# Row-half transposes and a new order of work inside the query steps of a fused attention and two-layer kernel

## The chip, the cores and the metric

One Trainium2 chip, and of it one core. The time is device microseconds of one launch; the kernel before took 869.48 us (median of 3 runs, 868.94 to 870.9).

## The reference, cut to what matters

Linear attention with random features, and behind it two feed-forward layers on the 2304 tokens that come out. The change lies in the attention, in the part that works on the queries.

```python
batch, n_heads, seq, head_dim, n_features = 4, 8, 576, 64, 128
def phi(x):                                   # x is q or k, times 64 ** -0.25
    proj = einsum('bhsd,md->bhsm', x, omega)
    sq = sum(x * x, axis=-1, keepdims=True) / 2
    h = proj - sq
    return exp(h - max(h, axis=-1, keepdims=True)) / sqrt(128)
q_p, k_p = phi(q), phi(k)
kv = einsum('bhsm,bhsd->bhmd', k_p, v);  z = sum(k_p, axis=2)
out = einsum('bhsm,bhmd->bhsd', q_p, kv) / (einsum('bhsm,bhm->bhs', q_p, z) + 1e-6)
x = out.transpose(0, 2, 1, 3).reshape(2304, 512)
x = leaky(x @ moe_w_in) @ moe_w_out           # d_ff = 2048, a slope for each hidden unit
return relu(x @ moe2_w_in) ** 2 @ moe2_w_out
```

## The kernel before, in words

The 2304 tokens are 18 tiles of 128. The key steps come first (`k_step`, 18 and a tail), then the query steps (`q_step`, numbered s = 0 to 20), then the two layers, which fill the time from about 136 us on. Every engine's instructions run in the order in which the code records them, so the order of lines in `q_step` is the order on each engine. Between the query steps' own instructions `make()` records pieces of the preparation of the layers' weights (on ACT, DVE, POOL and the DMA queues). In the last steps, from s = 18 (`DRAIN`), `more()` adds the first products of the layers; before that it does nothing.

A query step is a software pipeline over four tiles of tokens. In step s:

- DVE divides the products of tile z = s - 3 by their denominator (L723 to L725, `rec` and `xn`).
- PE transposes the 8 heads' features of tile v = s - 2, `eq`, 128x128 each: the first four into the PSUM bank `tt[0]`, the next four into `tt[1]` (L735). ACT copies each bank to SBUF (`t`, L738, two copies of 512 columns).
- ACT takes the exponentials of tile s - 1 (L637, eight of 128 columns).
- PE projects tile s (L612): eight products with a contraction of 64 rows, which alternate between the upper and the lower half of PE's rows. DVE takes the maxima over them (L625, `greatest`, 1024 columns).
- PE transposes the divided outputs `xn` of tile z into `tt[0]` (L754, four of 128x128), and DVE copies them into `x` (L755, 512 columns).
- PE sums the squares of tile s into 8 columns of `tt[1]` (L619, 64 output rows at a time). DVE makes of these and the maxima the bias of the next step's exponentials (L631 and L632, `bias`).
- PE multiplies tile v's transposed features with the sums over keys (L767, 16 products of 64 output rows, into `o`).

`tt[0]` and `tt[1]` are one PSUM bank each and are never doubled: the transposes of `eq`, those of `xn` and the sums of squares take turns in them, and each must wait until ACT or DVE has read what stood there. The projections have two sets of banks in turn, `o` has one.

Of the kernel before, what the change touches and what calls it, by code (L numbers as in the profile page):

```python
# [9 lines left out]
F32 = mybir.dt.float32  # L10
# [9 lines left out]
P = 128  # L20
B, H, S, D = 4, 8, 576, 64
T = B * S
NT = T // P
NP = H // 2
# [3 lines left out]
KC = DM // P  # L28
# [3 lines left out]
W = D + 1  # L32
# [22 lines left out]
DRAIN, DRAINED = 18, 6  # L55
# [5 lines left out]
def tile_performer_moe(ctx, tc, qt, kt, qn, kn, vn, omt, w1i, w1o, al, w2i, w2o, out):  # L61
    nc = tc.nc
# [467 lines left out]
    def xpart(t0, n):  # L530

        b = t0 // NB
        assert (t0 + n - 1) // NB == b
        return x[:, b, :, t0 - b * NB:t0 - b * NB + n]

    def attention():
        with ExitStack() as ac:
            ka = ac.enter_context(tc.tile_pool(name="ka", bufs=1, side="right"))
            ld = ac.enter_context(tc.tile_pool(name="ld", bufs=4, side="right"))
            wk = ac.enter_context(tc.tile_pool(name="wk", bufs=3, side="right"))  # L540
# [11 lines left out]
            tt = [po.tile([P, 512], F32, name=f"t{j}") for j in range(2)]  # L552
# [5 lines left out]
            def projections(i):  # L558

                j = i % 2  # L560
                if halves_only[j]:
                    halves_only[j].close()
                    halves_only[j] = None
                    pools[j] = (pbc, ac)[j].enter_context(
                        tc.tile_pool(name=("pb", "pa")[j], bufs=1, space=PSUM, reuse_waits="tile", **sides[j]))
                return pools[j].tile([P, 2, NP, M], F32, name="h")

            def products():
                return po.tile([P, 2, 512], F32, name="o")

            HP = P // 2
            HALVES = (slice(0, HP), slice(HP, P))
            om = ka.tile([P, M], F32, name="om")
            pick = ka.tile([P, 2], F32, name="pick")
            ident = ka.tile([P, P], F32, name="ident")
            kvr = ka.tile([P, B, H, W], F32, name="kvr")
# [13 lines left out]
            def load(key):  # L590
                which, i = key
                raws[key] = raw = ld.tile([P, NP, P], F32, name="raw")
                nc.sync.dma_start(out=raw, in_=(kt if which == "k" else qt)[i])
# [5 lines left out]
            def square(key):  # L599
                sqts[key] = wk.tile([P, NP, P], F32, name="sqt", bufs=2)  # L600
                nc.gpsimd.tensor_tensor(out=sqts[key], in0=raws[key], in1=raws[key], op=ALU.mult)
# [6 lines left out]
            def project(key, pj):  # L608

                for c in range(NP):  # L610
                    for j, rows in enumerate(HALVES):
                        nc.tensor.matmul(pj[j][:, c, :] if isinstance(pj, list) else pj[:, j, c, :], raws[key][rows, c, :], om[rows], start=True, stop=True)  # L612

            def square_sums(key, o):

                sqt = sqts.pop(key)
                for c in range(NP):
                    for rows in HALVES:
                        nc.tensor.matmul(o[rows, 2 * c:2 * c + 2], sqt[:, c, rows], pick,  # L619
                                         start=True, stop=True, skip_group_check=True)  # L620
                return o.rearrange("p (c j) -> p j c", j=2)

            def greatest(pj, n=2):
                mx = sm.tile([P, 2, NP], F32, name="mx")[:, :n]
                nc.vector.reduce_max(out=mx, in_=pj, axis=AX.X)  # L625
                return mx

            def bias(mx, nsq, n=2):

                nb = sm.tile([P, 2, NP], F32, name="nb")[:, :n]  # L630
                nc.vector.tensor_tensor(out=mx, in0=nsq, in1=mx, op=ALU.add)  # L631
                nc.vector.tensor_tensor(out=nb, in0=nsq, in1=mx, op=ALU.subtract)  # L632
                return nb

            def feature(pj, nb, e):
                for c in range(NP):
                    nc.scalar.activation(out=e[:, c, :], in_=pj[:, c, :], func=AF.Exp, bias=nb[:, c:c + 1])  # L637
# [28 lines left out]
            has = lambda i, n=NT: 0 <= i < n  # L666
# [44 lines left out]
            fs, ns, qpj, qnb, outs = {}, {}, {}, {}, {}  # L711

            def q_step(s, make=lambda: None, more=lambda: None):
                k = next(ahead, None)
                if k:
                    load(k)

                z = s - 3
                if has(z):
                    o = outs.pop(z)[:, :, 0:NP * W].rearrange("p j (h w) -> p j h w", w=W)  # L720
                    ns[z] = xn = wk.tile([P, NP, 2, D], F32, name="xn", bufs=2)
                    rec = sm.tile([P, 2, NP, 1], F32, name="rec")
                    nc.vector.tensor_scalar(out=rec, in0=o[:, :, :, D:], scalar1=eps, scalar2=None, op0=ALU.add)  # L723
                    nc.vector.reciprocal(out=rec, in_=rec)
                    nc.vector.tensor_tensor(  # L725
                        out=xn.rearrange("p c j d -> p j c d"), in0=o[:, :, :, 0:D],
                        in1=rec.to_broadcast([P, 2, NP, D]), op=ALU.mult)
                make()

                v = s - 2  # L730
                if has(v):
                    e = fs.pop(v)
                    for j in range(2):
                        for c in range(NP):
                            nc.tensor.transpose(tt[j][:, c * P:(c + 1) * P], e[:, j, c], ident)  # L735
                    t = [wk.tile([P, NP, P], F32, name=f"t{j}", bufs=2) for j in range(2)]
                    for j in range(2):
                        nc.scalar.copy(out=t[j], in_=tt[j].rearrange("p (c n) -> p c n", n=P))  # L738
                if has(s - 1):
                    fs[s - 1] = e = wk.tile([P, 2, NP, M], F32, name="eq", bufs=2)  # L740
                    for j in range(2):
                        feature(qpj[s - 1][:, j], qnb[s - 1][:, j], e[:, j])
                    del qpj[s - 1], qnb[s - 1]
                more()
                if has(s):
                    qpj[s] = projections(s)
                    project(("q", s), qpj[s])
                    mx = greatest(qpj[s])

                if has(z):  # L750
                    xt = tt[0].rearrange("p (c n) -> p c n", n=P)
                    xn = ns.pop(z).rearrange("p c j d -> p c (j d)")
                    for c in range(KC):
                        nc.tensor.transpose(xt[:, c, :], xn[:, c], ident)  # L754
                    nc.vector.tensor_copy(out=xpart(z * P, P), in_=xt)  # L755
                more()

                if has(s):
                    nsq = square_sums(("q", s), tt[s % 2 if s < 2 else 1][:, 0:H])
                    qnb[s] = bias(mx, nsq)  # L760
                if has(v):
                    outs[v] = o = products()
                    for j in range(2):
                        for c in range(NP):
                            for rows in HALVES:
                                b = (v * P + rows.start) // S
                                nc.tensor.matmul(o[rows, j, c * W:(c + 1) * W], t[j][:, c, rows], kvr[:, b, 2 * c + j],  # L767
                                                 start=True, stop=True, skip_group_check=True)
                if has(s + 1):
                    square(("q", s + 1))  # L770

# [33 lines left out]
            for j in range(3):  # L805
                k_step(NT + j)
                q_step(j)
                if j < 2:
                    onward(1, BLOCKS - 1)
                else:  # L810
                    ask(2, BLOCKS - 1)
# [12 lines left out]
            for s in range(3, NT + 3):  # L824
                def make():
                    for n, at in zip((B11, B21, B12, B22), CASTS):
                        if s == at:
                            cast(0, n, as_it_is)
                        elif s == at + 1:
                            rest(0, n, as_it_is)  # L830
                    if s == HELD:
                        held.pop()()
                    if s in APART:
                        apart(APART[s])
                    if s == CAST:

                        gate[0] = len(UNITS) * 4
                        ask(2, 0)
                    blk = 0 if s >= CAST else BLOCKS - 1
                    upto(STAGES + MADE.get(s, 0), 2, blk)  # L840
                    if s == DRAIN:
                        apart(T4)
                    if s == DRAIN + 1:
                        cast(0, T2, in_place)
# [433 lines left out]
    def room_of(k, n):  # L1278
        return x[:, k].rearrange("p c n -> p (c n)")[:, n * NB:(n + 1) * NB]
# [145 lines left out]
    for c in range(3):  # L1425
        o = room_of(k, M65)[:, c * QW:(c + 1) * QW]
# [45 lines left out]
```

## Time and profile before

| | us |
|---|---|
| median of 3 runs | 869.48 (868.94 to 870.9) |
| profiled execution, its own time | 868.84 |
| its span, first to last instruction | 867.0 |
| query steps 3 to 17 in it, from step 3's first transpose to step 18's | 63.10 to 126.87 |
| PE busy | 862.3 (99%) |
| DVE busy | 677.6 (78%) |
| ACT busy | 520.6 (60%) |

The busy shares are over the whole span, of which the layers are five sixths. For the change only the query steps count, and of them the order of PE, DVE and ACT inside one step. A PE that counts as busy can still lose time between instructions of different shapes, since the recorded matmuls overlap each other.

### The profile page before, as it was taken

The page shows a single profiled execution, that of the slowest core. Times are in us where ns is not written, and L with a number is a line of the kernel's source. Part 1 is how long each engine was busy: PE and PEld are TensorE (multiplying, and loading weights), DVE is VectorE, ACT ScalarE, POOL GpSimd, SP SyncE. Part 2 cuts the span into 40 slices and gives each one's busy share as a digit, 9 for nine tenths or more (in the row PEclk, how much of TensorE's full clock was granted, in tenths as well). Part 3 has the DMA queues.
Part 4 walks back from the last instruction along what each step waited for, and adds up shares of the span by engine and source line. Part 5 has one row for each costly group of instructions (what it writes and reads, how often), then busy time and mean ns, then how long its engine had stood idle before and what let it go on. Part 6 is the DMA issues. An engine that isn't in the chain of part 4 may idle for free.

```text
span 867.0 us, 17497 instructions
## 1 busy us (share of the span) xinstructions
PE 862.3 (99%) x6803; PEld 799.1 (92%) x6803; DVE 677.6 (78%) x1126; ACT 520.6 (60%) x1027; POOL 97.3 (11%) x138
## 2 busy tenths in 40 slices
PE   9999999999999999999999999999999999999998
PEld 7998889999999999999999999998899988999888
DVE  5778987998996776888778865669956699757686
ACT  6889897999877666667767633335333355333442
POOL 6742432111101000010000000000000000000000
PEclk9999999999999999999999999999999999999999
DMA  7744306899838999839999957687797687876874
GB/s 260 218 151 149 112 14 232 290 323 332 313 125 273 395 381 379 314 112 380 394 406 383 360 197 226 217 293 252 255 309 250 207 311 257 300 253 224 299 254 153
DMA packets 88530, 228.76 MB, mean 264 GB/s; under 512 B 6784, under 2 KB 19456, under 8 KB 83456
## 3 DMA queue, kind: packets, MB, share of 16 engines
q1 hardware_dynamic: 78880, 192.21, 62.6%
q0 software_dynamic: 9216, 33.56, 11.4%
q10 hardware_dynamic: 352, 1.87, 0.6%
q8 instruction: 54, 0.88, 0.4%
q14 instruction: 28, 0.23, 0.1%
HBM read 170.47 MB, written 57.15 MB: 263 GB/s over the span
## 4 chain that ended last, share of the span: by engine, by line
PE 94%; ACT 2%; DVE 2%; DMA 1%; issue 0%; ACTq 0%; DVEq 0%
PE h L861 29%; PE y L1057 21%; PE sumc L1251 11%; PE spare L861 10%; PE suma L1251 9%; PE h L612 4%; PE t L735 2%; PE t L619 2%; PE o L767 2%; PE o L658 2%; PE t L754 1%; ACT e L637 1%; DMA x<-in_w2i 1%; DVE xl L498 0%; PE t L606 0%
## 5 line engine op out<-in xcount | busy, mean ns | idle before, releaser
L861 PE MATMUL h<-xh,w 128*128 128x384 f32 x984 | 276.2, 337 | 0.1
L861 PEld LDWEIGHTS h<-xh,w 128*128 128x128 f32 x984 | 180.4, 188 | 2.9 <-ACT c L886 0.4
L1057 PE MATMUL y<-gh,w 128*128 128x512 f32 (+1 forms) x768 | 174.1, 337 | 0.1
L861 PE MATMUL h<-xl,w 128*128 128x384 f32 x492 | 165.3, 336 | 0.0
L1057 PEld LDWEIGHTS y<-gh,w 128*128 128x128 f32 x768 | 130.6, 188 | 12.6 <-ACT gh L886 0.4
L1057 PE MATMUL y<-gl,w 128*128 128x512 f32 (+1 forms) x384 | 102.2, 337 | 0.0
L1266 ACT CAST gh<-g 128x768 fp32r<-128x768 f32 x72 | 56.9, 833 | 74.1 <-PE suma L1251 33.1
L861 PEld LDWEIGHTS h<-xl,w 128*128 128x128 f32 x492 | 92.5, 188 | 2.1
L861 PE MATMUL spare<-xh,w 128*128 128x384 f32 x336 | 91.0, 334 | 0.0
L1268 DVE TENSOR_TENSOR gl<-g,gh 128x768 fp32r<-128x768 f32 x72 | 65.7, 953 | 14.3 <-PE suma L1251 7.1
L1251 PE MATMUL sumc<-w,gh 128*128 128x512 f32 (+1 forms) x296 | 76.6, 379 | 0.0
L1057 PEld LDWEIGHTS y<-gl,w 128*128 128x128 f32 x384 | 67.1, 188 | 9.7
L886 ACT ACTIVATE s<-h,sg_sb 128x384 f32<-128x384 f32 x69 | 40.0, 580 | 37.8 <-PE h L861 37.6
L861 PEld LDWEIGHTS spare<-xh,w 128*128 128x128 f32 x336 | 61.3, 188 | 0.2
L1251 PEld LDWEIGHTS sumc<-w,gh 128*128 128x128 f32 x296 | 52.8, 189 | 9.3
L625 DVE TENSOR_REDUCE mx<-h 128x8 f32<-128x1024 f32 (+1 forms) x38 | 44.4, 1167 | 18.1 <-PE h L612 17.4
L899 DVE SCALAR_TENSOR_TENSOR c<-h,sg_sb,s 128x384 f32<-128x384 f32 x69 | 42.4, 615 | 18.0 <-PE h L861 7.2
L861 PE MATMUL spare<-xl,w 128*128 128x384 f32 x168 | 56.1, 334 | 0.0
L904 DVE SCALAR_TENSOR_TENSOR c<-c,al_sb 128x768 f32<-128x768 f32 x48 | 48.6, 1012 | 8.4 <-ACT c L886 8.4
L1251 PE MATMUL suma<-w,gh 128*128 128x512 f32 x216 | 52.4, 391 | 0.0
L886 ACT ACTIVATE gh<-c,sg_sb 128x768 fp32r<-128x768 f32 x48 | 45.0, 937 | 8.1 <-DVE c L904 7.9
L910 DVE SCALAR_TENSOR_TENSOR gl<-c,sg_sb,gh 128x768 fp32r<-128x768 f32 x48 | 48.5, 1011 | 0.0
(138 smaller groups left out, 1500.8 us busy)
## 6 DMA issues: line engine op xcount, KB each, us to landing
w<-k SPq DMA_DIRECT2D x99, 512.0 KB, 5.1
w<-k SPq DMA_DIRECT2D x39, 1024.0 KB, 4.9
w<-k SPq DMA_DIRECT2D x26, 896.0 KB, 7.7
k<-ms SPq DMA_DIRECT2D x36, 512.0 KB, 7.0
k<-w SPq DMA_DIRECT2D x16, 512.0 KB, 6.5
x<-in_w2i POOLq DMA_DIRECT2D x16, 512.0 KB, 6.5
x<-in_w2o POOLq DMA_DIRECT2D x16, 512.0 KB, 7.2
ms<-in_w1o POOLq DMA_DIRECT2D x14, 512.0 KB, 5.8
```

The lines of the kernel that those rows point to most:

```text
L612: nc.tensor.matmul(pj[j][:, c, :] if isinstance(pj, list) else pj[:, j, c, :], raws[key][rows, c, :], om[rows], start=True, stop=True)
L619: nc.tensor.matmul(o[rows, 2 * c:2 * c + 2], sqt[:, c, rows], pick, start=True, stop=True, skip_group_check=True)
L625: nc.vector.reduce_max(out=mx, in_=pj, axis=AX.X)
L861: nc.tensor.matmul(out, w[:, u, a, cs], tiles[v, b][:, kc], start=start and kc == 0 and j == 0, stop=stop and kc == 1 and j == 2, skip_gro ...
L886: nc.scalar.mul(out=to, in_=of, mul=sg_sb[:, 2 * p + i:2 * p + i + 1])
L899: nc.vector.scalar_tensor_tensor(out=c[:, ts], in0=b, scalar=sign, in1=s, op0=ALU.mult, op1=ALU.add)
L904: nc.vector.scalar_tensor_tensor(out=c, in0=c, scalar=slope, in1=c, op0=ALU.mult, op1=ALU.max)
L910: nc.vector.scalar_tensor_tensor(out=gl[:, i], in0=c, scalar=sign, in1=gh[:, i].bitcast(F32), op0=ALU.mult, op1=ALU.subtract)
L1057: nc.tensor.matmul(y[a0 // 512][:, a0 % 512:a0 % 512 + a1 - a0], u[:, i, c * P:(c + 1) * P], v[:, i, ts], start=first and j == 0 and a0 % ...
L1251: nc.tensor.matmul(to[c] if v == 3 or banks else to[c][:, :QW], (l if v == 2 else h)[:, r, c * P:(c + 1) * P], both(r) if v == 3 else w[:, ...
L1266: nc.scalar.copy(out=h[:, r], in_=f[:, r])
L1268: nc.vector.tensor_tensor(out=l[:, r], in0=f[:, r], in1=h[:, r].bitcast(F32), op=ALU.subtract)
```

## The change

Four edits, all in the query steps; the key steps keep their form (the squares of keys are still summed in halves).

1. Up to s = 17 the transposes of `eq` and of `xn` are made in row halves: each 128x128 transpose becomes two with a contraction of 64 rows, whose outputs are 128x64. The upper halves go to `tt[0]`, the lower ones to `tt[1]`, in turn. ACT still copies both banks, and DVE copies `xn`'s out of both, 256 columns each.
2. The products with the sums over keys stand in front of the sums of squares.
3. The query's sums of squares are made in quarters (32 output rows) where they were made in halves.
4. The transposes of `xn` and the copies of them into `x` stand in front of the maxima.

From s = 18 on the forms and the order are as before.

```diff
             def square_sums(key, o):
 
                 sqt = sqts.pop(key)
+                n = P // 2 if key[0] == "k" else P // 4
                 for c in range(NP):
-                    for rows in HALVES:
+                    for rows in (slice(r, r + n) for r in range(0, P, n)):
                         nc.tensor.matmul(o[rows, 2 * c:2 * c + 2], sqt[:, c, rows], pick,
                                          start=True, stop=True, skip_group_check=True)
...
                     e = fs.pop(v)
+                    t = [wk.tile([P, 512], F32, name=f"t{j}", bufs=2) for j in range(2)]
                     for j in range(2):
                         for c in range(NP):
-                            nc.tensor.transpose(tt[j][:, c * P:(c + 1) * P], e[:, j, c], ident)
-                    t = [wk.tile([P, NP, P], F32, name=f"t{j}", bufs=2) for j in range(2)]
+                            if s < DRAIN:
+                                at = slice((j * NP + c) * HP, (j * NP + c + 1) * HP)
+                                for r, rows in enumerate(HALVES):
+                                    nc.tensor.transpose(tt[r][:, at], e[rows, j, c], ident[rows, rows])
+                            else:
+                                nc.tensor.transpose(tt[j][:, c * P:(c + 1) * P], e[:, j, c], ident)
                     for j in range(2):
-                        nc.scalar.copy(out=t[j], in_=tt[j].rearrange("p (c n) -> p c n", n=P))
+                        nc.scalar.copy(out=t[j], in_=tt[j])
+
+                    def turned(j, c, r):
+
+                        if s < DRAIN:
+                            return t[r][:, (j * NP + c) * HP:(j * NP + c + 1) * HP]
+                        return t[j][:, c * P + r * HP:c * P + (r + 1) * HP]
...
                     project(("q", s), qpj[s])
+
+                if has(z):
+                    xn = ns.pop(z).rearrange("p c j d -> p c (j d)")
+                    if s < DRAIN:
+                        xt = [tt[r][:, 0:2 * P].rearrange("p (c n) -> p c n", n=HP) for r in range(2)]
+                        for c in range(KC):
+                            for r, rows in enumerate(HALVES):
+                                nc.tensor.transpose(xt[r][:, c], xn[rows, c], ident[rows, rows])
+                        for r in range(2):
+                            nc.vector.tensor_copy(out=xpart(z * P + r * HP, HP), in_=xt[r])
...
+                more()
+                if has(s):
                     mx = greatest(qpj[s])
 
-                if has(z):
-                    xt = tt[0].rearrange("p (c n) -> p c n", n=P)
-                    xn = ns.pop(z).rearrange("p c j d -> p c (j d)")
-                    for c in range(KC):
-                        nc.tensor.transpose(xt[:, c, :], xn[:, c], ident)
-                    nc.vector.tensor_copy(out=xpart(z * P, P), in_=xt)
-                more()
-
-                if has(s):
-                    nsq = square_sums(("q", s), tt[s % 2 if s < 2 else 1][:, 0:H])
-                    qnb[s] = bias(mx, nsq)
                 if has(v):
                     outs[v] = o = products()
...
-                                nc.tensor.matmul(o[rows, j, c * W:(c + 1) * W], t[j][:, c, rows], kvr[:, b, 2 * c + j],
+                                nc.tensor.matmul(o[rows, j, c * W:(c + 1) * W], turned(j, c, r), kvr[:, b, 2 * c + j],
                                                  start=True, stop=True, skip_group_check=True)
+                if has(s):
+                    nsq = square_sums(("q", s), tt[s % 2 if s < 2 else 1][:, 0:H])
+                    qnb[s] = bias(mx, nsq)
```

On PE, step 10 of the kernel before, from the transposes of `xn` to the next step's transposes of `eq` (`t_129` is `tt[0]`, `t_130` is `tt[1]`, `t_1944` and `t_1945` are ACT's copies of them):

```order
L754 MATMUL t_129<-ident,xn 128x128 [waits DVE_49,Activation_49]
L754 MATMUL t_129<-ident,xn 128x128 x3
L619 MATMUL t_130<-pick,sqt 64x2 [waits Activation_49,Pool_49]
L619 MATMUL t_130<-pick,sqt 64x2 x7
L767 MATMUL o<-kvr,t_1944 64x65 [waits PE_49]
L767 MATMUL o<-kvr,t_1944 64x65 x7
L767 MATMUL o<-kvr,t_1945 64x65 x8
L735 MATMUL t_129<-ident,eq 128x128 [waits DVE_49,Activation_49]
L735 MATMUL t_129<-ident,eq 128x128 [waits Activation_49] x3
L735 MATMUL t_130<-ident,eq 128x128 [waits DVE_49,Activation_49]
```

The sixteen products stand between the sums of squares and the next transposes, and of those the first that writes `tt[1]` is the fifth.

The same place of the changed kernel (`t_2115` and `t_2116` are ACT's copies there):

```order
L768 MATMUL t_129<-ident,xn 128x64 [waits DVE_49,Activation_49]
L768 MATMUL t_130<-ident,xn 128x64 [waits Activation_49]
...
L786 MATMUL o<-kvr,t_2115 64x65 [waits PE_49]
L786 MATMUL o<-kvr,t_2116 64x65
...
L620 MATMUL t_130<-pick,sqt 32x2 [waits DVE_49,Pool_49]
L620 MATMUL t_130<-pick,sqt 32x2 x15
L740 MATMUL t_129<-ident,eq 128x64 [waits Activation_49]
L740 MATMUL t_130<-ident,eq 128x64 [waits DVE_49]
```

The sums of squares now stand last in the step, the second transpose of the next step writes `tt[1]` and waits for DVE, and the second transpose of `xn` writes `tt[1]` too and waits for ACT.

On DVE, step 11 of the kernel before, from its last instruction for the weights or the casts (L498) to the next step's `xn`:

```order
L498 TENSOR_TENSOR xl_1384<-x,xh_1383 128x768
L625 TENSOR_REDUCE mx<-h 128x8 [waits PE_49]
L755 COPY x<-t_129 128x4x128 [waits PE_49,Activation_49]
L631 TENSOR_TENSOR mx<-t_130,mx 128x8 [waits DVE_49,PE_49,Activation_49]
L632 TENSOR_TENSOR nb<-t_130,mx 128x8 [waits DVE_49]
L723 TENSOR_SCALAR rec<-o 128x8 [waits PE_49]
```

The maxima wait for the projections and run while PE makes the transposes of `xn`; the copy comes after them.

The same place of the changed kernel:

```order
L498 TENSOR_TENSOR xl_1416<-x,xh_1415 128x768
L770 COPY x<-t_129 128x4x64 [waits PE_49,Activation_49]
L770 COPY x<-t_130 128x4x64 [waits PE_49,Activation_49]
L626 TENSOR_REDUCE mx<-h 128x8
L632 TENSOR_TENSOR mx<-t_130,mx 128x8 [waits DVE_49,PE_49]
L633 TENSOR_TENSOR nb<-t_130,mx 128x8 [waits DVE_49]
```

The two copies wait for the transposes of `xn`, and the maxima stand behind them.

## Rows read from the trace of the kernel before

**Rows 1.** The page: span; busy time by engine; granted TensorE clock in 40 slices.

```profile
span 867.0 us, 17497 instructions
PE 862.3 (99%) x6803; PEld 799.1 (92%) x6803; DVE 677.6 (78%) x1126; ACT 520.6 (60%) x1027; POOL 97.3 (11%) x138
PEclk9999999999999999999999999999999999999999
```

**Rows 2.** Busy time in steps 3 to 17; first line names the columns.

```profile
core 0: us, PE busy (x) PEld busy (x) DVE busy (x) ACT busy (x) POOL busy (x), PEclk, DMA share, GB/s
63.10:126.87 63.77, 63.77 (x1144) 55.92 (x1140) 56.01 (x123) 56.28 (x167) 22.66 (x21) 1.00 0.31 105
```

**Rows 3.** Chain of waits, 108 to 118 us: start, length, engine and work.

```profile
by line: PE o L767 25.4%; PE h L612 21.8%; PE t L735 20.5%; PE t L754 17.6%; PE t L619 16.9%
...
109.94 1.02 PE t L735 x8
110.96 1.09 PE h L612 x16
112.05 0.59 PE t L754 x4
112.64 0.56 PE t L619 x16
113.20 0.99 PE o L767 x32
```

**Rows 4.** Timeline of PE: transposes that begin steps 2, 3 and 18.

```profile
59.42 1.11 PE L735 MATMUL t<-ident,eq 128*128 128x128 f32 x8
...
63.10 1.09 PE L735 MATMUL t<-ident,eq 128*128 128x128 f32 x8
...
126.87 1.09 PE L735 MATMUL t<-ident,eq 128*128 128x128 f32 x8
```

**Rows 5.** Timeline of PE, step 10: start, length, line, weights' shape, moving shape.

```profile
92.86 1.09 PE L735 MATMUL t<-ident,eq 128*128 128x128 f32 x8
93.89 1.16 PE L612 MATMUL h<-om,raw 64*128 64x128 f32 x16
94.98 0.66 PE L754 MATMUL t<-ident,xn 128*128 128x128 f32 x4
95.56 0.63 PE L619 MATMUL t<-pick,sqt 128*64 128x2 f32 x16
96.05 1.13 PE L767 MATMUL o<-kvr,t 128*64 128x65 f32 x32
97.11 0.44 PE L735 MATMUL t<-ident,eq 128*128 128x128 f32 x2
```

**Rows 6.** Timeline of DVE, step 10.

```profile
93.42 0.69 DVE L725 TENSOR_TENSOR xn<-o,rec 128x512 f32<-128x512 f32 x1
94.02 0.95 DVE L498 TENSOR_TENSOR xl<-x,xh 128x768 fp32r<-128x768 f32 x1
95.09 1.23 DVE L625 TENSOR_REDUCE mx<-h 128x8 f32<-128x1024 f32 x1
96.23 0.68 DVE L755 COPY x<-t 128x512 f32<-128x512 f32 x1
96.83 0.16 DVE L631 TENSOR_TENSOR mx<-t,mx 128x8 f32<-128x8 f32 x1
97.02 0.17 DVE L632 TENSOR_TENSOR nb<-t,mx 128x8 f32<-128x8 f32 x1
97.23 0.17 DVE L723 TENSOR_SCALAR rec<-o 128x8 f32<-128x8 f32 x1
```

**Rows 7.** Timeline of ACT, step 10.

```profile
93.56 1.07 ACT L738 COPY t<-t 128x512 f32<-128x512 f32 x2 [0.38 <-PE t L735]
94.52 2.19 ACT L637 ACTIVATE eq<-h,nb 128x128 f32<-128x128 f32 x8
```

**Rows 8.** Groups of DVE and ACT, 63 to 127 us: count, busy us, mean ns.

```profile
L625 DVE TENSOR_REDUCE mx<-h 128x8 f32<-128x1024 f32 x15 | 18.4, 1225 | 5.6 <-PE h L612 4.9
L755 DVE COPY x<-t 128x512 f32<-128x512 f32 x15 | 10.2, 681 | 0.0
...
L738 ACT COPY t<-t 128x512 f32<-128x512 f32 x30 | 16.1, 589 | 6.7 <-PE t L735 6.7
```

More of the change, by code (lines that the diff above doesn't have):

```diff
@@ L747, in q_step @@
                     project(("q", s), qpj[s])
-                    mx = greatest(qpj[s])
                 if has(z):
-                    xt = tt[0].rearrange("p (c n) -> p c n", n=P)
                     xn = ns.pop(z).rearrange("p c j d -> p c (j d)")
-                    for c in range(KC):
-                        nc.tensor.transpose(xt[:, c, :], xn[:, c], ident)
-                    nc.vector.tensor_copy(out=xpart(z * P, P), in_=xt)
+                    if s < DRAIN:
[5 more added lines that the diff above has]
+                            nc.vector.tensor_copy(out=xpart(z * P + r * HP, HP), in_=xt[r])
+                    else:
+                        xt = tt[0].rearrange("p (c n) -> p c n", n=P)
+                        for c in range(KC):
+                            nc.tensor.transpose(xt[:, c, :], xn[:, c], ident)
+                        nc.vector.tensor_copy(out=xpart(z * P, P), in_=xt)
                 more()
                 if has(s):
-                    nsq = square_sums(("q", s), tt[s % 2 if s < 2 else 1][:, 0:H])
-                    qnb[s] = bias(mx, nsq)
+                    mx = greatest(qpj[s])
                 if has(v):
@@ L764, in q_step @@
                         for c in range(NP):
-                            for rows in HALVES:
+                            for r, rows in enumerate(HALVES):
                                 b = (v * P + rows.start) // S
-                                nc.tensor.matmul(o[rows, j, c * W:(c + 1) * W], t[j][:, c, rows], kvr[:, b, 2 * c + j],
+                                nc.tensor.matmul(o[rows, j, c * W:(c + 1) * W], turned(j, c, r), kvr[:, b, 2 * c + j],
                                                  start=True, stop=True, skip_group_check=True)
+                if has(s):
+                    nsq = square_sums(("q", s), tt[s % 2 if s < 2 else 1][:, 0:H])
+                    qnb[s] = bias(mx, nsq)
                 if has(s + 1):
```

## The prediction

> **What bounds the kernel now.** I read the page first: one core, PE busy 99% of 867.0 us, its clock granted in full in every slice [rows 1]. That says little on the query steps, so I cut out steps 3 to 17. There PE has no idle time at all, DVE is busy 56.0 and ACT 56.3 of 63.8 us [rows 2]. The chain of waits in this stretch is PE alone, phase after phase [rows 3]. From step 3's first transpose to step 18's are 63.77 us [rows 4], 15 equal periods of 4.25 us.
>
> One period by the starts of its phases [rows 5], all in us: transposes of eq 1.03 (92.86 to 93.89), projections 1.09, transposes of xn 0.58, sums of squares 0.49, products 1.06. So PE sets the period. But DVE has little room beside it: the maxima start at 95.09, 0.11 after the projections' phase ends, and maxima, copy into x and the bias's two operations end at 97.19; the transposes that overwrite what the copy and the bias read begin at 97.11 in tt[0] and about 0.45 later in tt[1] [rows 5, 6]. The maxima run beside xn's transposes, and the copy and the bias beside the products. That cover is what the new order moves.
>
> **The change, part by part.** The phases give the price of a transpose: eight take 1.03 and four 0.58, so one takes 0.1125 and each phase has a constant of 0.13. The projections show row halves of the same weight shape: 8 products, recorded as 16 rows of 64x128, in 1.09 [rows 5]. If the two halves run side by side that is 8 pairs at 0.12 with the same constant. A pair of row halves then costs what one whole transpose costs, and edit 1 gains nothing by itself except constants: transposes, projections and xn's transposes have one shape now, so of the four changes of shape in a step three are left, at about 0.13 to 0.19 each.
>
> Edit 3: the sums of squares take 0.031 a row with 2 moving columns, the products 0.033 with 65 [rows 5]; so time goes with the 64 weight columns. No row shows 32 columns. Bounds: the phase of 0.49 falls to 0.25 if four run side by side at half the time, or doubles to 0.98 if only two do. Taken is 0.25 to 0.49, and it will not matter, since PE waits for DVE at this place in any case.
>
> What matters is the order. I follow one period from T = 0, the start of the first transpose of eq into tt[1]. It waits for the bias's second operation, since the bias reads the sums in tt[1]; before, the first transpose that did so was the fifth, and the products stood between.
>
> - ACT's first copy started 0.70 after the first of four transposes into its bank (92.86 to 93.56) [rows 5, 7]. Now a bank is complete only with the seventh or eighth pair, 3 to 4 pairs later: 1.10.
> - ACT's two copies take 1.07 [rows 7]: 2.17. With 0.05 for the waking (the first copy before starts that long after its last transpose ended) 2.22. Here the second xn transpose, which writes tt[1], may start. PE has been ready since about 1.8 (8 and 8 pairs at 0.1125): a new wait of 0.4. Before, xn's transposes wrote tt[0] alone, which ACT's first copy frees early.
> - From the projections' start to the maxima's start are 1.20 for 8 pairs (93.89 to 95.09) [rows 5, 6]. Without four pairs, without the last tt[1] half, and with 64 instead of 128 columns to drain, xn's transposes to the first DVE copy take 0.63: 2.85.
> - The copy of 512 columns is followed by the next instruction after 0.60 and lasts 0.68, an operation of 8 columns lasts 0.16 [rows 6]; on the line between them 256 columns last 0.42, and 0.34 pass to the next instruction. Bounds are 0.30 (half of 0.60) and 0.60 (no saving). Two copies: 3.53.
> - The maxima now start only here. They take 1.14 to the next instruction (95.09 to 96.23) [rows 6], and each of the 15 is alike, 1225 ns in the mean [rows 8]: 4.67.
> - Bias: 0.19 and 0.17 [rows 6]: 5.03. PE's waking on DVE is not seen before; between 0 and 0.15, I take the 0.05 of ACT on PE: 5.08, and the next period starts.
>
> PE's own rest (products 1.06, change of shape, sums 0.25 to 0.49) ends at about 4.3 and is covered by the maxima. DVE's xn and what it does for the weights end some 2.1 us after the bias and are covered by PE and ACT. ACT's exponentials need 2.19, from 2.1 to 4.3, and up to 0.8 us of casts behind them fit before its next copy at 6.2. The DMA queues get more time in each step than before, and POOL's squares are a step ahead.
>
> So 5.08 against 4.25, 0.83 more in each of the steps 3 to 17: 15 x 0.83 = 12.4. Step 2 has no xn; it takes 3.68 from transposes to transposes [rows 4]. Its products wait for ACT's second copy (2.22), then 1.06, the sums 0.13 + 0.25 to 0.49, 0.11, the bias 0.36 and 0.05: some 4.2, or +0.5. Against that stand step 18, whose first four transposes write tt[0] alone and need not wait for the bias (up to -0.45), and steps 0 and 1, with cheaper sums (0 to -0.2 each). These I let cancel. Behind step 18 the chain is PE's and no phase there is held by anything that a later start would hide, so all of it reaches the end. The execution profiled took 868.84, of which 867.0 are span: 868.84 + 12.4 = 881.2. The median of the runs shown is 0.64 above that execution, so the forecast is **881.9 us**, 1.4% slower.
>
> **The rivals.**
>
> *PE stays the bound (faster).* If the chain of copies, maxima and bias were hidden, the period would be PE's sum: 0.90 + 0.90 + 0.45 + 0.93 (the products without their constant) + 0.25, and three changes of shape at 0.13 to 0.19, some 3.85. That is 0.40 x 15 = 6.0 less: 863.5. For it speaks that the chain of waits is PE's now [rows 3]. It decides if copies, maxima and bias (0.68 + 1.14 + 0.36 = 2.2) fit beside the products, the sums and two constants (1.5 to 1.7); they don't, and the order shows the wait. 3%.
> The Trainium skill, "TensorEngine Tiling (Array Packing)", Key Properties, says that a change of the tiling mode drains the engine; the constants agree with it. By that rule alone the change gains, one change of mode a step.
>
> *Halves that pack twice as well.* If a pair cost half of a whole transpose, because its moving side has half the columns, the phase of eq's transposes loses 0.45 and that of xn's 0.22: a period of 4.4, 15 x 0.17 = 2.5, hence 872. Against it: 2 and 65 moving columns cost the same [rows 5]. 7%.
> The same page, Theoretical Speedup, gives up to 2x for a contraction of 64 rows or less; the projections' rows bear out that two halves go side by side, not that a pair is cheaper than a whole transpose.
>
> *Halves that don't run side by side.* 16 and 8 transposes at 0.1125 would put 0.9 and 0.4 into the period: 6.3 or so, +31: about 900. The projections' rows speak against it, but they are products, not transposes. 8%.
>
> *The clock falls.* PE now waits about 1.2 us of each 5.1, which it never did in this stretch [rows 2]. At 1.2 GHz the phases on the path (0.8 + 0.4, and the drains) double: +1.3 a step, 901. In the slice at the start, where PE was not always busy, the clock was granted in full too [rows 1]. 3%.
>
> *Less than I see:* a wait that is released earlier than I read it, copies at 0.30 and constants that vanish: between 867 and 873. 5%.
>
> **How the numbers follow.** The forecast has 74%. Its own range: copies of 0.30 to 0.60, durations that don't overlap as they did (up to 0.3 a step), waking of 0 to 0.15, and 0.1 either way in the phases of eq's and xn's transposes give periods of 4.9 to 5.6, so +10 to +20 and, with the small steps, 878 to 891. The range down to the packing rival and up to a tail of the forecast, 872 to 894, holds a little over 80%; the serial halves and the clock lie above, the PE rival below. A measurement of this kernel tells 0.2%, 1.7 us, from no change. Faster by more: the PE rival and a little of the others, 4%. Within: 4%. Slower: 92%.
>
> **What would show it.** In the profile after, PE has idle time in each query step, of about 0.4 in front of the transposes of xn, ended by ACT's copies, and of about 0.7 in front of those of eq, ended by the bias on DVE. The starts of eq's transposes are 5.1 apart. The chain of waits in this stretch goes through DVE's maxima and ACT's copies. The two DVE copies show about 420 ns each, and the copies by ACT start some 1.1 after eq's transposes begin in earnest. 16 transposes take about as long as 8 did. From 140 us on, all is the kernel before, shifted. I am wrong if the period stays at 4.25 or less, if PE's idle time in the stretch is nil, or if the loss comes from slower transposes or a lower clock rather than from the two waits.

## The result, and the profile after

Four runs of the changed kernel have a median of 879.01 us (877.9 to 879.92), the kernel before 869.21 beside them: a ratio of 1.011 [1.0097, 1.0123], 9.8 us slower. The forecast was 881.9 in a range of 872 to 894. The profiled run of the changed kernel took 879.92, the highest of the four.

I read the same views as before, the page first:

```profile
span 878.1 us, 18448 instructions
PE 856.9 (98%) x7279; PEld 793.6 (90%) x7279; DVE 679.8 (77%) x1141; ACT 519.6 (59%) x1027; POOL 97.0 (11%) x138
PEclk9999999999999999999999999999999999999999
```

Against [rows 1], PE was busy for 5.4 us less in a span 11.1 us longer, at the same clock: PE waits. The busy times from step 3's transposes to step 18's (columns as in [rows 2]):

```profile
64.03:135.65 71.62, 56.92 (x1570) 49.86 (x1560) 57.49 (x136) 55.65 (x167) 23.27 (x21) 1.00 0.28 93
```

The 15 periods take 71.62 instead of 63.77, nearly all of them 4.77 instead of 4.25 (the first two are 4.59 and 4.48, and one is 5.32, in which PE stops for 0.30 in the middle of the transposes of `eq`, for nothing that the profile shows). PE, which had no idle time here, is busy 56.92. The waits in this stretch (who waits, for whom, us in all, times, the longest in us) name two places:

```profile
PE t L740 <- DVE nb L633: 11.5, 15, 0.8
PEld t L768 <- ACT t L744: 5.3, 15, 0.4
PE t L768 <- ACT t L744: 2.8, 15, 0.2
```

One period on PE, step 10, to be laid beside [rows 5]:

```profile
98.60 0.71 PE L740 MATMUL t<-ident,eq 64*128 64x64 f32 x15 [0.82 <-DVE nb L633]
99.09 1.17 PE L612 MATMUL h<-om,raw 64*128 64x128 f32 x16
100.04 0.22 PE L768 MATMUL t<-ident,xn 64*128 64x64 f32 x1
100.45 0.46 PE L768 MATMUL t<-ident,xn 64*128 64x64 f32 x7 [0.19 <-ACT t L744]
100.83 1.15 PE L786 MATMUL o<-kvr,t 128*64 128x65 f32 x32
101.92 0.43 PE L620 MATMUL t<-pick,sqt 128*32 128x2 f32 x32
102.28 0.27 PE L740 MATMUL t<-ident,eq 64*128 64x64 f32 x1
103.37 0.40 PE L740 MATMUL t<-ident,eq 64*128 64x64 f32 x6 [0.82 <-DVE nb L633]
```

The first half of `eq` into `tt[0]` may start (102.28); the second, into `tt[1]`, waits for the bias. DVE and ACT in the same period, for [rows 6, 7]:

```profile
100.96 0.75 DVE L770 COPY x<-t 128x256 f32<-128x256 f32 x2 [0.51 <-ACT eq L638]
101.63 1.22 DVE L626 TENSOR_REDUCE mx<-h 128x8 f32<-128x1024 f32 x1
102.95 0.17 DVE L632 TENSOR_TENSOR mx<-t,mx 128x8 f32<-128x8 f32 x1
103.15 0.17 DVE L633 TENSOR_TENSOR nb<-t,mx 128x8 f32<-128x8 f32 x1
```

```profile
99.32 1.07 ACT L744 COPY t<-t 128x512 f32<-128x512 f32 x2 [0.90 <-PE t L740]
```

The copies begin when the transposes of `xn` end (100.91); the "ACT eq" in brackets is an inferred releaser, and the wrong one. The maxima now start 2.54 after the projections do, instead of 1.20. Copies, maxima and bias follow one another from 100.96 to 103.33, and PE has only the products, the sums and one half of `eq` to put beside them. The chain of waits, 98 to 108 us, has passed from PE alone to DVE most of all:

```profile
by line: DVE mx L626 34.3%; issue 18.8%; PE t L740 14.6%; ACT t L744 12.5%; ACT eq L638 10.7%; DVE x L770 9.4%; DVE mx L632 5.3%; DVE nb L633 5.3%; DVEq L632 0.6%
```

The span's 11.1 us are 7.85 in steps 3 to 17, 0.09 in step 2 (3.77 against 3.68), 0.72 between the transposes of steps 18 and 19 (5.38 against 4.66; the second four there wait 0.52), 0.84 ahead of step 2 and 1.6 at a weight tile that arrives late:

```profile
155.13 0.68 ACT L137 ACTIVATE ms<-ms 128x512 f32<-128x512 f32 x1 [1.59 <-DMA ms<-in_w1i]
```

From there on the kernel is the one before, shifted by a constant 11.1. The 0.84 and the 1.6 rest on one profiled run, and both vary among the runs below: step 2 begins 0.72 and 0.20 us later than before in eq_halves and late_save, whose code is alike up to there, and the wait for that weight tile, nil in order_only, is 1.0 in sums_first. Whether any of them belongs to the change is open.

### The profile page after: what moved, and what is told of

Read it like the earlier page. It is cut to its first block, busy times and chain, and to the rows that moved or that the text cites. A ratio compares the mean times of both kernels' runs of the same rounds, so it can differ in the third digit from the quotient of the medians.

```text
span 878.1 us, 18448 instructions
## 1 busy us (share of the span) xinstructions
PE 856.9 (98%) x7279; PEld 793.6 (90%) x7279; DVE 679.8 (77%) x1141; ACT 519.6 (59%) x1027; POOL 97.0 (11%) x138
## 3 DMA queue, kind: packets, MB, share of 16 engines
q0 software_dynamic: 9216, 33.56, 11.1%
q10 hardware_dynamic: 352, 1.87, 0.5%
## 4 chain that ended last, share of the span: by engine, by line
PE 86%; DVE 6%; ACT 5%; issue 2%; DMA 1%; POOL 0%; ACTq 0%; DVEq 0%
PE h L883 27%; PE y L1079 20%; PE sumc L1273 11%; PE spare L883 10%; PE suma L1273 9%; PE h L612 2%; DVE mx L626 2%; PE o L659 2%; PE t L740 1%; PE t L620 1%; ACT t L744 1%; ACT eq L638 1%; DVE x L770 1%; DMA ms<-in_w1i 1%; ACT e L638 1%
## 5 line engine op out<-in xcount | busy, mean ns | idle before, releaser
L1079 PEld LDWEIGHTS y<-gh,w 128*128 128x128 f32 x768 | 130.7, 188 | 12.4 <-ACT gh L908 0.4
```

The lines of the kernel that those rows point to most:

```text
L1079: nc.tensor.matmul(y[a0 // 512][:, a0 % 512:a0 % 512 + a1 - a0], u[:, i, c * P:(c + 1) * P], v[:, i, ts], start=first and j == 0 and a0 % ...
```

## The experiments

The theory was that of the prediction, the order: with the maxima behind the copies (edit 4), copies, maxima and bias stand in a row. Its rivals were that the sums standing last (edit 2) make the loss, or the halves themselves. The medians are those of runs beside the kernel before on the same chip (869.71, 869.99 and 869.79 us in the three sets); a period is one query step in the middle of steps 3 to 17.

**max_first**: the changed kernel without edit 4's move of the maxima.

```diff
                     project(("q", s), qpj[s])
+                    mx = greatest(qpj[s])
...
-                if has(s):
-                    mx = greatest(qpj[s])
```

> The changed kernel with edit 4 taken back: the maxima stand again directly behind the projections, in front of the transposes of xn and their copies; halves, quarters and products in front of the sums stay. Theory A (one chain sets the period of 4.77: ACT's second copy, xn's transposes in tt[1], DVE's two copies, maxima, bias, eq's next transposes; the maxima behind the copies are what is new on it): the maxima start at about 1.6 after eq's transposes and end beside ACT's copies and xn's transposes, the copies end at 3.4, the sums behind the products end at 3.8, bias and waking 0.42: a period of about 4.2, so 15 x -0.05, 868 to 870 us, as before the change. Rival B (what costs is that the sums of squares stand last, so that the bias can't be hidden): the order of the products is kept, so 878 to 879. Rival C (the row halves and the quarters themselves cost): 878 to 879.

Measured: 880.17, ratio 1.0122 [1.0107, 1.0137]: no gain, and my expectation missed. The period is 4.65 to 4.72, hardly below 4.77. PE's timeline shows why:

```profile
97.43 0.43 PE L620 MATMUL t<-pick,sqt 128*32 128x2 f32 x32 [0.40 <-DVE x L771]
98.36 0.71 PE L740 MATMUL t<-ident,eq 64*128 64x64 f32 x15 [0.29 <-DVE nb L633]
```

With the maxima first, DVE's copies out of `tt[0]` and `tt[1]` come after them; the sums write `tt[1]`, where the lower halves of `xn` still stand, and wait for the second copy, and the bias waits for the sums. I had not followed that bank. Late in this profile the wait for the copy grows to 1.26, the granted clock is 0.93 between 110 and 125 us, and three steps take 5.3 to 5.9: a few us of the 880 are the clock's.

**sums_first**: the changed kernel without edit 2.

```diff
+                if has(s):
+                    nsq = square_sums(("q", s), tt[s % 2 if s < 2 else 1][:, 0:H])
+                    qnb[s] = bias(mx, nsq)
                 if has(v):
                     outs[v] = o = products()
...
-                if has(s):
-                    nsq = square_sums(("q", s), tt[s % 2 if s < 2 else 1][:, 0:H])
-                    qnb[s] = bias(mx, nsq)
```

> The changed kernel with edit 2 taken back: the sums of squares and the bias stand again in front of the products; halves, quarters and the copies in front of the maxima stay. Theory A: the maxima still start behind the copies, at about 3.0 after eq's transposes, and the bias behind them at 4.35, whatever PE does: period 4.75 to 4.8, the time of the changed kernel, 878 to 880 us. The sums wait for DVE's copy out of tt[1] (3.1), the products stand behind them and end at about 4.65, so they don't matter yet. Rival B (sums that stand last): the products cover the bias again, period 4.25 or less, 869 us or less.

Measured: 880.25, 1.0123 [1.0108, 1.0138], period 4.77, as expected (from 98 us on; before that five steps are longer, and between 90 and 100 the granted clock is 0.83). By its period the place of the sums is worth nothing while the maxima are late.

**halves_quarters**: both moves undone; what is left of the change is edits 1 and 3.

> The changed kernel with edits 2 and 4 taken back: row halves and quarters alone, in the order of before. Theory A, with the turns in tt[1] (xn's lower halves stand there now, so the sums of squares must wait until DVE has copied them out, and the products stand behind the sums): maxima 1.6 to 2.7 after eq's transposes, copies 2.7 to 3.45, sums 3.5 to 3.9, products to 5.0: a period of about 5.0, 15 x 0.75 = 11 more than before, 879 to 881 us. PE would stand still in front of the sums, waiting on DVE's copy. Rival B (the new order is the whole cost): period 3.8, 862 to 864 us.

Measured: 904.92, 1.0404 [1.0384, 1.0425], far over what I expected. The wait is the one I expected, in the last whole step at the full clock (first row) and after:

```profile
67.40 0.52 PE L620 MATMUL t<-pick,sqt 128*32 128x2 f32 x32 [1.33 <-DVE x L771]
...
95.50 1.91 PE L612 MATMUL h<-om,raw 64*128 64x128 f32 x16
97.25 0.41 PE L769 MATMUL t<-ident,xn 64*128 64x64 f32 x8
99.50 0.43 PE L620 MATMUL t<-pick,sqt 128*32 128x2 f32 x32 [1.84 <-DVE x L771]
```

The size is not: behind that step the granted clock falls. Two stretches of all engines (the number behind POOL's count is the granted clock):

```profile
60.00:70.00 10.00, 8.01 (x225) 7.44 (x227) 7.61 (x18) 7.90 (x24) 3.02 (x4) 1.00 0.51 177
90.00:100.00 10.00, 6.32 (x158) 5.94 (x156) 6.04 (x13) 6.76 (x21) 1.04 (x1) 0.81 0.18 53
```

A mean of 0.81 is a mixture of 2.4 and 1.2 GHz: in the trace the first stretch at 1.2 begins at 73.3 us, and from there to 162 us the two take turns. The projections take 1.91 instead of 1.17 and most periods 5.9 to 6.6. The one whole period at the full clock is 5.38; 15 of them would have cost some 17 us (an estimate, 15 x 1.13), the measured loss is 35.

**order_only**: the kernel before with the two moves alone, transposes whole (the reverse of the two diffs above).

> The kernel before with edits 2 and 4 alone: products in front of the sums of squares, copy of xn's transposes in front of the maxima; whole transposes, sums in halves. Theory A: from eq's first transpose into tt[1], which waits for the bias: four transposes 0.5, projections 1.1, xn's transposes and the start of the copy 0.7, copy 0.60, maxima to bias 1.32, bias and waking 0.42: a period of about 4.65, 15 x 0.4 = 6 more than before, 874 to 877 us. Rival C (halves and quarters cost, the order is free): 868 to 870 us.

Measured: 879.27, 1.0109 [1.0092, 1.0126], period 4.88 where I expected 4.65 (874 to 877 us); no single step of my sum has the difference, five are 0.01 to 0.09 longer. The order alone, without one half or quarter, costs the whole loss. DVE and PE of one step:

```profile
95.45 0.69 DVE L754 COPY x<-t 128x512 f32<-128x512 f32 x1 [0.66 <-PE t L753]
96.06 1.22 DVE L625 TENSOR_REDUCE mx<-h 128x8 f32<-128x1024 f32 x1
97.41 0.17 DVE L631 TENSOR_TENSOR mx<-t,mx 128x8 f32<-128x8 f32 x1
97.61 0.17 DVE L632 TENSOR_TENSOR nb<-t,mx 128x8 f32<-128x8 f32 x1
```

```profile
97.92 0.63 PE L735 MATMUL t<-ident,eq 128*128 128x128 f32 x4 [0.49 <-DVE rec L723]
```

Here four transposes fill part of PE's wait and 0.49 are left, but the four behind the bias take 0.56 where the sixteen halves take 0.49.

**xn_whole**: the changed kernel with the transposes of `xn` whole and in `tt[0]`, which takes the first wait away.

```diff
-                        xt = [tt[r][:, 0:2 * P].rearrange("p (c n) -> p c n", n=HP) for r in range(2)]
...
+                    xt = tt[0].rearrange("p (c n) -> p c n", n=P)
+                    for c in range(KC):
+                        nc.tensor.transpose(xt[:, c, :], xn[:, c], ident)
+                    nc.vector.tensor_copy(out=xpart(z * P, P), in_=xt)
```

> The changed kernel with one thing taken back: the transposes of xn are whole again and stand in tt[0] alone, with one copy of 512 columns; halves of eq, quarters, and the new order stay. It takes away the wait of xn's transposes for ACT's second copy, and leaves the maxima behind the copy. Theory A (that wait is worth the 0.2 to 0.4 by which xn's second transpose is held, the rest of the loss is copy, maxima and bias in series): xn's transposes start at 1.6 after eq's, copy at 2.3, maxima at 2.9, bias at 4.2, next period at 4.6, so 15 x 0.16 = 2.4 less than the changed kernel, 876 to 877 us. Rival (both waits are needed for the loss; without the first one the cover returns): 4.25 or less, 869 us or less.

Measured: 878.1, 1.0093 [1.0079, 1.0107], a period of 4.73. The wait for ACT is worth 0.04 a step and not the 0.16 that I expected: the whole transposes take as long as halves and wait together, 1.86 from the projections' start to the first copy against 1.87 (99.09 to 100.96).

**eq_halves**: halves_quarters with `xn` as in xn_whole, so that the sums wait for no copy: edits 3 and the half of 1 that concerns `eq`, in the order of before.

> Row halves for eq and quarters for the squares, but xn whole in tt[0], and the order of before (maxima, copy; sums of squares, products). Theory A: nothing of xn stands in tt[1], so the sums wait for ACT alone and run at 2.2, the products cover the copy and the bias, maxima start at 1.6 after eq's transposes, copy 2.75, bias 3.35, next period 3.75 to 3.9 (PE's own sum is 0.49 + 1.0 + 0.58 + 0.43 + 1.09 = 3.6 with a change of shape or two more): 15 x -0.35 to -0.5, that is 862 to 865 us, faster than before the change. PE busy, with at most some 0.2 of waiting a step. Rival (row halves don't pay where DVE and ACT have 3.3 to 3.8 of work in each step already): 4.1 to 4.25, 867 to 869 us.

Measured: 868.12, 0.998 [0.997, 0.9989], not the 862 to 865 that I expected and inside the rival's range. Yet most periods are near what I expected, 3.84 to 3.96 (93.81 to 97.72 below); two steps took 5.0 and 5.5:

```profile
93.81 0.89 PE L740 MATMUL t<-ident,eq 64*128 64x64 f32 x16
94.48 1.17 PE L612 MATMUL h<-om,raw 64*128 64x128 f32 x16
95.58 0.66 PE L767 MATMUL t<-ident,xn 128*128 128x128 f32 x4
96.17 0.43 PE L620 MATMUL t<-pick,sqt 128*32 128x2 f32 x32
96.53 1.15 PE L780 MATMUL o<-kvr,t 128*64 128x65 f32 x32
97.72 0.89 PE L740 MATMUL t<-ident,eq 64*128 64x64 f32 x16
```

In such a step PE is at work throughout again. Before late_save I put the two long steps down to query tiles that land late, and the trace says otherwise. In the one of 5.0 PE stops for 1.09 with 28 of the 32 rows of one tile's sums behind it. In the one of 5.5 it stops for 1.47 between the first and the second weight load of the projections (`PEld`), and the first already reads the step's tile, which was issued at 62.37 and landed 5.7 later:

```profile
77.18 0.19 PEld L612 LDWEIGHTS h<-om,raw 64*128 64x128 f32 x1
78.94 0.97 PEld L612 LDWEIGHTS h<-om,raw 64*128 64x128 f32 x15 [1.56 <-issue]
```

"issue" says that the profile shows nothing that PE waited for. Beside this stop runs the first save of prepared weights; between 60 and 85 us its issue and those of the query tiles are (count, KB each, median us to landing):

```profile
k<-w ACTq DMA_DIRECT2D x1, 1792.0 KB, 8.7
raw<-in_qt SPq DMA_DIRECT2D x6, 256.0 KB, 4.0
```

**quarters_alone**: the kernel before with edit 3.

```diff
+                n = P // 2 if key[0] == "k" else P // 4
-                    for rows in HALVES:
+                    for rows in (slice(r, r + n) for r in range(0, P, n)):
```

> The kernel before with edit 3 alone: the query's sums of squares in quarters. Before, PE sets the period of 4.25 without any wait. In the changed kernel the sums take 0.36 with their change of shape counted to the next phase, before 0.49; but the products behind them now have another shape than the sums, which costs one change more, about 0.1. Theory A: -0.05 to 0 a step, 868 to 870 us, no difference that can be measured. Rival (quarters are worth their full 0.13 a step): 867 us.

Measured: 868.85, 0.9982 [0.9967, 0.9998], a period of 4.17. The sums' phase falls from 0.49 to 0.36, of which 0.08 a step arrive: between the 0.05 of my theory and the 0.13 of the rival.

**uppers_first**: eq_halves with all 8 upper halves ahead of all 8 lower ones.

```diff
+                        for r, rows in enumerate(HALVES):
+                            for j in range(2):
+                                for c in range(NP):
```

> The kernel eq_halves with the sixteen half transposes of eq in another order: the eight of the upper rows first, then the eight of the lower, where they alternated. Only the price of a half is asked. In the changed kernel sixteen in turn took 0.49, 0.031 each. If two halves run side by side and each costs about half of a whole one for its 64 moving columns, then without the turn each costs 0.056 and the phase lasts 0.9 to 1.0. If a half is cheap by itself, the phase stays near 0.5. The first copy by ACT starts after eight halves in either case.

One run: 869.16. From the first half to the first of the projections (87.24 to 87.82) are 0.58, where I expected 0.9 to 1.0 or some 0.5: from 87.52 on the trace has lower halves start beside the last upper ones, though they stand behind them in the code. What the run tells is how the halves start. The x in the brackets counts the transposes under way in a stretch of 0.02 us; the first ends only after 0.22. Here, the first upper halves, one after the other:

```profile
87.32:87.34 0.02, 0.02 (x2) 1.00 1.34 512
87.38:87.40 0.02, 0.02 (x3) 1.00 0.00 0
87.44:87.46 0.02, 0.02 (x4) 1.00 0.03 0
```

and in the changed kernel, upper and lower in turn:

```profile
98.60:98.62 0.02, 0.02 (x2) 1.00 0.00 0
98.70:98.72 0.02, 0.02 (x4) 1.00 0.00 0
98.76:98.78 0.02, 0.02 (x6) 1.00 0.00 0
```

One more each 0.06 us there, two more here (the first gap is 0.10). A half costs 0.06, half of a whole (0.1125), and two of different row halves start together: 0.03 a half when alternated.

**edit2_only** and **edit4_only**: eq_halves with one of the two moves each, to separate the edits in a form without the bank conflict of max_first.

> eq_halves (halves of eq, quarters, xn whole in tt[0], order of before) with edit 2 alone put in: products in front of the sums of squares, maxima still in front of the copy. Nothing of xn stands in tt[1] here, so no turn in that bank holds the sums. Theory A (each of the two moves costs by itself, because it takes a cover away): from eq's first transpose into tt[1], 0.49 + 1.10 + 0.58 + 1.09 to the start of the sums (durations of the runs so far), 0.50 to the bias, 0.42 to the next such transpose: 4.18 a step against 3.87 in eq_halves, 13 to 15 steps x 0.31 = 4 to 4.6 more than eq_halves, 871 to 873 us. Rival (only the maxima behind the copy cost, and in max_first it was the bank): as eq_halves, 867 to 869 us.

> eq_halves with edit 4 alone put in: the copy of xn's transposes in front of the maxima, sums of squares still in front of the products. Theory A: copy at 2.25 after eq's first transpose into tt[1], maxima at 2.85, bias 1.32 later, next such transpose 0.42 later: 4.6 a step against 3.87, 13 to 15 steps x 0.72 = 9 to 11 more than eq_halves, 876 to 879 us; with both edits xn_whole took 4.73. Rival (the products cover the maxima, since they stand behind the sums): at most 4.25, 869 to 872 us.

Measured: 872.09, 1.0027 [1.0016, 1.0038], period 4.25, and 876.52, 1.0081 [1.0068, 1.0094], period 4.73. Both as expected. (The profiled execution of edit2_only is its slowest, 877.0: PE stops for 1.38 in the middle of one step's projections, and the granted clock is 0.65 between 85 and 92 us behind it. The period is read after that.) With eq_halves and xn_whole this is a table of four:

```
                          sums before products    products before sums
maxima before copies      868.1  (3.87)           872.1  (4.25)
copies before maxima      876.5  (4.73)           878.1  (4.73)
```

Edit 4 is the dear one. Behind it the period is the chain projections, `xn`'s transposes, copy, maxima, bias, and the move of the sums adds nothing to the period. Alone, the sums' move costs because they end with PE's row, and the bias (0.4) then stands between them and the next transposes; PE's wait in edit2_only:

```profile
100.65 0.71 PE L740 MATMUL t<-ident,eq 64*128 64x64 f32 x15 [0.28 <-DVE nb L633]
```

**late_save**: eq_halves with the first save of prepared weights, beside which the longer stop falls, seven steps later.

```diff
-HELD = 5
+HELD = 12
```

> eq_halves with one transfer moved: the first weight save of 1.8 MB (on ACT's queue) is issued in step 12 in place of step 5. In eq_halves' trace two steps are long, 5.03 and 5.54 where the others take 3.85 to 3.95: the query tiles' loads land late, in the second case beside this save, which took 8.7 us. If that is where part of the gain of eq_halves went, step 6 falls to 3.9: -1.5, 866 to 867 us; the step of 5.03 (weight reads of POOL's queue) stays. If it isn't, no change, 868 us.

Measured: 865.76, 0.996 [0.9947, 0.9973]. The step of 5.5 falls to 3.85, and between 60 and 85 us the tiles now land in 2.6:

```profile
raw<-in_qt SPq DMA_DIRECT2D x6, 256.0 KB, 2.6
```

So the stop goes with the save, but not through the query tile, as I had it: that tile had been in SBUF for 9 us. The trace offers another way, which no run here tests: a transfer of the instruction queue (q8 in the page) starts at 76.50 beside the save in eq_halves and at 72.32 in late_save, and PE may have stood for its instructions. This version is faster than both kernels, 4 us below the one before. One step of 5.0 us is left in it.

## Why the prediction was right

By its own steps, for one period from the first transpose of `eq` into `tt[1]` (98.60) to the next (103.37):

```
                                          predicted   measured
transposes of eq -> ACT's first copy         1.10       0.72
ACT's two copies                             1.07       1.07
waking, second transpose of xn               0.05       0.06
-> first DVE copy                            0.63       0.51
two DVE copies                               0.68       0.67
maxima -> bias                               1.14       1.32
bias's two operations, waking                0.41       0.42
period                                       5.08       4.77
```

- The mechanism was right: both waits, at the two places named, 15 times each, the one on ACT at 0.2 of PE's time (0.4 predicted) and the one on DVE's bias at 0.8 (0.7 predicted); the clock stayed full; the chain runs through the maxima.
- Mis-sized: "A pair of row halves then costs what one whole transpose costs." It costs half of that. The 16 halves take 0.49 and not 0.9 and more, and the copies by ACT start 0.38 earlier; the same term shortens the way to the first DVE copy by 0.12. I had taken the price from the projections, whose halves have 128 moving columns, and these have 64. Rows with 2 and 65 moving columns cost the same [rows 5], which made me set this rival at 7%. Its price of a half was right; its 872 us were not: of the 0.67 a step that it took off, 0.50 came, and the next point went the other way. Whether the moving side or the weights set the price of a half is not shown.
- The other way, 0.18: before, a copy stood between maxima and bias and the start of the copy 1.14 after that of the maxima hid that the bias needs their result. Now the dependent operation starts 1.32 after them, their 1.22 and 0.1 more.
- So the steps cost 7.85 and not 12.4. That the total is only 2.9 below the forecast is in part luck: in the profiled execution 3.2 of the 11.1 us lie outside these steps, where I let everything cancel. Step 2 gave +0.09 (predicted +0.5). Step 18 was forecast at up to -0.45 and measured at +0.72: its second four transposes wait for DVE all the same. The 0.84 and the 1.6 were not in the sum.
- Edit 3's phase fell to 0.36, inside its bounds of 0.25 to 0.49, and did not matter, as the prediction said; alone it is worth 0.08 a step.
- "Edit 1 gains nothing by itself except constants" failed with the mis-sized term. Halves of `eq` with quarters, in the old order, give a period of 3.87. The rival "PE stays the bound" had 3.85, by other terms: 0.90 for the transposes of `eq`, which take 0.67 there, and halves for `xn`, which is whole there. The change has this gain in it and its order hides it.

The Trainium skill, "TensorEngine Tiling (Array Packing)", Theoretical Speedup, gives up to twice the rate for a contraction of 64. The starts above agree for the halves that take turns: two each 0.06 instead of one.

The first wait is real and nearly free, which the prediction did not see: it counted the wait as a part of the sum, and xn_whole, which has none, is 0.04 a step shorter. A wait in a chain is worth only what the next longest chain leaves of it.

## What to carry to other kernels

Before an operation is moved behind another on a busy engine, ask what it needs: the maxima needed the projections alone, and behind the copies they started 1.3 us later, all of it on the path of the next step. Follow the banks as well as the engines: between halves_quarters and eq_halves, in the same order, the halves of `xn` in a bank that a copy had still to read made some 37 us, the lower clock included. A phase that gets shorter on the bound engine shows its gain only if nothing else stops that engine: moving one large save brought some 2 of the 4 us that late_save gains. And before a long step is put down to a load that is on its way, look where in the step the engine stops, and whether what it works on there had landed.

## What the runs showed of the hardware

- A transpose of a 64x128 row half started 0.06 us after the one before it in the same row half, a whole one some 0.11; halves of different rows started together.
- Sums with 32 weight columns started in fours, a new four each 0.03 us, with 64 columns in twos, each 0.06. The phases took 0.36 for 32 rows and 0.49 for 16, changes of shape included.
- PE's waits of 0.8 and 0.2 in a period of 4.77 left the granted clock at 1.0; in halves_quarters PE waited 1.33 and 1.41 for a copy, and 0.2 each for ACT, in the two periods before the clock first fell, and up to 2.5 after; the mean there was 0.76 between 81 and 160 us.
- A DVE operation that reads the result of the one before started 0.1 us after its end behind the maxima, and 0.03 to 0.04 after it in the bias and the division; an independent one started 0.09 before that end (1.14 after the start of one that lasts 1.23).
- PE stopped inside a phase, for nothing that the profile shows: 0.30 us (the changed kernel), 1.09 and 1.47 (eq_halves), 1.38 (edit2_only). The 1.47 went when the weight save was moved.
